# First two columns in one load, first up matmuls ahead of column 1's gate, other spin counts

## The chip, the cores and the metric

One core of a Trainium2 chip runs the kernel. The metric is device time in microseconds (us). The kernel before takes about 178.5 us. The profile's span starts and ends a little inside the measured time (176.9 of 178.62 us in one run).

Engine names: PE is TensorE, PEld its weight loads, DVE is VectorE, ACT ScalarE, POOL GpSimd, SP SyncE, whose queue ("SPq") issues nearly all loads.

## The reference, cut to what matters

```python
x  = A_x                                   # 1 x 2048 x 512, bf16
xn = _layernorm(x, axis=-1)
# A: rfft2, product with a complex weight, irfft2        (not touched here)
# B: h = gelu(xn @ w_gate) * (xn @ w_up);  h @ w_down    (512 -> 1792 -> 512)
return x + _A_ref(xn, A_w_r, A_w_i) + _B_ref(xn, B_w_gate, B_w_up, B_w_down)
```

The kernel works in 16 "columns" of 128 rows. A column is loaded, normalised and transposed; then gate and up matmuls take it through weights that are still arriving.

## The kernel before

The loads, in the order in which SyncE issues them:

```python
pin(load_x(0, 1))                  # column 0
pin(load_x(1, 1))                  # column 1
idx_t = pc.tile([P, 3], I32, name="idx_t")
nc.sync.dma_start(out=idx_t[:], in_=nc.inline_tensor(idx_np, name="spec_rows").ap())  # index table
load_w(Wg_sb, 0, 512)              # first gate weights
load_w(Wu_sb, 0, 512)              # first up weights
load_x(2, 2)
for e in range(0, NE, 2):
    load_w(Wg_sb, 512, 1024, e=slice(e, e + 2))
load_w(Wu_sb, 512, 1024)           # second up block
load_x(4, 4)
# ... more weights, columns 8 to 15, tables
```

The index table is read by gathers late in the kernel. TensorE runs dummy matmuls ("spins") until there is work, so that its array is at full pace (in the trace spins start every 107 ns up to 4.87 us and every 56 ns from 5.86 us on):

```python
for k in range(37):
    pin(nc.tensor.matmul(sp_ps[:, :P], lhsT=spin[:], rhs=spin[:], start=True, stop=True))

def spin_on():                      # after column 0's transposes
    for k in range(11):
        nc.tensor.matmul(sp_ps[:, :P], lhsT=spin[:], rhs=x_t[:, 0, :P], start=True, stop=True)
```

The first units of work: `k == 0` is column 0 and `k == 1` column 1 with the first weights, `k == 2` and `k == 3` are both columns with the second block. `LAND`, `WG_LAND` and `WU_LAND` are landing times assumed by a list scheduler in the source; `key` orders the operations of an engine.

```python
if k == 0:
    g = add("PE", occ / 4, lambda: mm_part(0, 1), [xT_op[0, 0]], key=1000, acq=("G",), t_min=WG_LAND[0])
    between["t", 0].deps.append(g)                 # column 1's transposes come between
    g = add("PE", occ / 4, lambda: mm_part(1, 2), [g, between["t", 1]], key=1000.1)
    g = add("PE", occ / 2, lambda: mm_part(2, NE), [xT_op[0], g], key=1000.2, lat=occ / 2 + 0.3)
# ...
u = split("u_ps", "U", Wu_sb, (1001.4, 1001.5, 1003.1, 1003.5)[k] if k < 4 else 1000.5 + k, WU_LAND, ...)
```

So TensorE's order was: gate of column 0 (with column 1's transposes inside), gate of column 1, up of column 0, up of column 1, then 256-wide gate matmuls for both columns, transposes of columns 2 and 3, 256-wide up matmuls.

## Time and profile before

| | before |
|---|---|
| time, median of 3 runs | 178.56 us (178.42 to 178.85) |
| PE busy | 172.8 of 176.9 us |
| first gate matmul | 6.66 us |
| first 256-wide gate matmul | 10.47 us |
| last matmul | 173.93 us |

The page's first part gives each engine's busy time, its share of the span and its instructions:

```profile
span 176.9 us, 3143 instructions
## 1 busy us (share of the span) xinstructions
PE 172.8 (98%) x1150; PEld 96.9 (55%) x1150; DVE 115.9 (66%) x255; ACT 96.0 (54%) x171; POOL 17.2 (10%) x38
```

PE has almost no idle time left, so a gain has to come from the few us before the real matmuls start. The timeline of PE from 5 us shows them; columns are start, length, engine, line, operation, tiles, shapes and count, and in brackets the idle time before with what ended it:

```profile
...
5.42 0.61 PE L351 MATMUL tp<-ident_t,xn 128*128 128x128 bf16 x4 [0.24 <-DVE xn L345]
5.86 0.78 PE L324 MATMUL sp_ps<-x_t,spin 128*128 128x128 bf16 x11
6.66 0.40 PE L502 MATMUL g_ps<-xnT,Wg_sb 128*128 128x128 bf16 x4
6.90 0.39 PE L351 MATMUL tp<-ident_t,xn 128*128 128x128 bf16 x4
7.12 1.73 PE L502 MATMUL g_ps<-xnT,Wg_sb 128*128 128x128 bf16 x28
...
```

The waits of PEld name what the first gate weights waited for (total us, times, longest):

```profile
PEld L320 <- DVE minus_half L266: 1.0, 1, 1.0
PEld L351 <- DVE xn L345: 0.7, 2, 0.5
PEld L502 <- DMA Wg_sb<-in_B_w_gate_dram: 0.2, 1, 0.2
```

The reader should see two chains that race to 6.66 us: column 0 (load, statistics, normalise, transposes, spins) and the landing of the gate weights. The weights lost, by 0.2 us: the last spin starts at 6.42 us and the first gate matmul, 0.045 us behind the landing of its weights, at 6.66.

### The profile page before, as it was taken

The numbers are of one execution on the slowest core, as the hardware profiler recorded it, in microseconds if no ns is written. First come the engines' busy times: TensorE is split into PE (matmuls) and PEld (weight loads), VectorE is DVE, ScalarE is ACT, GpSimd is POOL, SyncE is SP. The second block draws the span as 40 slices with busy tenths as digits, with TensorE's granted clock in tenths as the row PEclk, the third lists the DMA queues.
The fourth block names the chain that finished last, engine by engine and source line by source line (L and its number), as shares of the span: only waits on it lengthen the run. The fifth ranks groups of instructions, "written<-read, shape, count | busy, mean of one in ns | idle before, by whom it ended". The sixth has DMA issues, their size and how long they took to land.

```text
span 176.9 us, 3143 instructions
## 1 busy us (share of the span) xinstructions
PE 172.8 (98%) x1150; PEld 96.9 (55%) x1150; DVE 115.9 (66%) x255; ACT 96.0 (54%) x171; POOL 17.2 (10%) x38
## 2 busy tenths in 40 slices
PE   7999999999999999999999999999999999999993
PEld 7798845455545554555555455454445445444463
DVE  2588999987434599979899999643516325345333
ACT  3452489799736988898899965362112111211200
POOL 1020340506760000000000000000000000000000
DMA  3999999233717802211201510200122221221212
GB/s 99 323 387 377 371 199 151 60 64 71 246 41 238 299 0 59 59 30 35 59 19 42 152 47 15 59 0 4 59 89 89 77 75 60 89 88 60 82 40 59
DMA packets 21743, 19.35 MB, mean 109 GB/s; under 512 B 8480, under 2 KB 20000, under 8 KB 21728
## 3 DMA queue, kind: packets, MB, share of 16 engines
q1 hardware_dynamic: 21312, 17.84, 36.4%
q0 software_dynamic: 416, 1.32, 2.6%
q8 instruction: 9, 0.15, 0.4%
q14 instruction: 6, 0.05, 0.1%
HBM read 13.38 MB, written 2.10 MB: 87 GB/s over the span
## 4 chain that ended last, share of the span: by engine, by line
PE 95%; DVE 2%; DMA 1%; issue 0%
PE u_ps L494 27%; PE y_ps L829 27%; PE g_ps L494 25%; PE g_ps L502 2%; PE bp L589 2%; PE yp L780 2%; PE gp L750 2%; PE dp L647 2%; PE y_ps L833 2%; PE ep L656 2%; DMA x_t<-in_A_x_dram 1%; DVE stats L339 1%; PE tp L351 1%; DVE xn L345 0%; DVE xnT L354 0%; DVE y_sb L836 0%
## 5 line engine op out<-in xcount | busy, mean ns | idle before, releaser
L494 PE MATMUL u_ps<-xnT,Wu_sb 128*128 128x512 bf16 (+2 forms) x272 | 57.1, 341 | 0.0
L494 PE MATMUL g_ps<-xnT,Wg_sb 128*128 128x512 bf16 (+1 forms) x224 | 53.3, 364 | 0.0
L829 PE MATMUL y_ps<-Wd_sb,hT 128*128 128x512 bf16 (+2 forms) x252 | 51.1, 355 | 0.0
L512 DVE TENSOR_TENSOR hT<-u_ps,ge 128x512 bf16<-128x512 f32 x56 | 38.4, 688 | 18.1 <-PE u_ps L494 16.5
L507 ACT ACTIVATE ge<-g_ps 128x512 bf16<-128x512 f32 x56 | 33.5, 601 | 22.3 <-PE g_ps L494 18.3
L494 PEld LDWEIGHTS <-Wu_sb 128*128 128x128 bf16 x272 | 24.8, 98 | 20.7
L829 PEld LDWEIGHTS <-hT 128*128 128x128 bf16 x252 | 23.2, 98 | 22.4
L494 PEld LDWEIGHTS <-Wg_sb 128*128 128x128 bf16 x224 | 21.5, 98 | 20.5
L786 ACT CAST yf<-yp 128x512 bf16<-128x512 f32 x16 | 9.3, 586 | 40.5 <-PE yp L780 40.5
L836 DVE TENSOR_TENSOR y_sb<-y_ps,y_sb 128x512 bf16<-128x512 f32 (+2 forms) x18 | 11.1, 632 | 30.0 <-PE y_ps L833 30.0
L661 ACT CAST E<-ep 64x512 bf16<-64x512 f32 x32 | 18.5, 579 | 1.4 <-PE ep L656 1.0
L339 DVE BATCH_NORM_STATS2 stats<-x_t 128x6 f32<-128x512 bf16 x16 | 10.4, 674 | 3.9 <-DMA x_t<-in_A_x_dram 3.9
L456 ACT ACTIVATE xn<-x_t,nb,rstd 128x512 bf16<-128x512 bf16 x12 | 9.5, 812 | 1.0 <-POOL nb L370 1.0
L559 ACT CAST ds<-dp 128x512 bf16<-128x512 f32 x16 | 9.2, 597 | 0.8 <-PE dp L647 0.8
L559 ACT CAST Gs<-gp 128x512 bf16<-128x512 f32 x16 | 8.7, 591 | 0.6 <-PE gp L750 0.5
L559 ACT CAST Bs<-bp 128x512 bf16<-128x512 f32 x16 | 8.3, 606 | 0.5 <-PE bp L589 0.5
L792 DVE TENSOR_TENSOR lv<-yf 128x512 bf16<-128x512 bf16 x16 | 6.1, 421 | 1.5 <-ACT yf L786 0.6
L780 PEld LDWEIGHTS <-Gs 128*128 128x128 bf16 x64 | 4.8, 98 | 3.5
L799 DVE TENSOR_TENSOR yt<-lv 128x512 bf16<-128x512 bf16 x16 | 6.1, 421 | 0.3
L833 PE MATMUL y_ps<-yt,RI_t 128*128 128x512 bf16 (+2 forms) x18 | 6.1, 355 | 0.0
L780 PE MATMUL yp<-CT,Gs 128*128 128x128 bf16 x64 | 6.0, 219 | 0.0
L571 DVE TENSOR_TENSOR A<-xn 128x1024 bf16<-128x1024 bf16 x8 | 5.2, 676 | 1.0 <-ACT xn L456 1.0
(65 smaller groups left out, 125.5 us busy)
## 6 DMA issues: line engine op xcount, KB each, us to landing
F<-F SPq DMA_DIRECT2D x32, 64.0 KB, 2.0
y_sb<-in_A_x_dram SPq DMA_DIRECT2D x16, 128.0 KB, 2.1
out_dram<-y_sb SPq DMA_DIRECT2D x15, 128.0 KB, 1.7
Wd_sb<-in_B_w_down_dram SPq DMA_DIRECT2D x1, 1792.0 KB, 7.6
x_t<-in_A_x_dram SPq DMA_DIRECT2D x5, 256.0 KB, 9.8
Wu_sb<-in_B_w_up_dram SPq DMA_DIRECT2D x2, 512.0 KB, 6.2
Wg_sb<-in_B_w_gate_dram SPq DMA_DIRECT2D x1, 768.0 KB, 10.2
Wu_sb<-in_B_w_up_dram SPq DMA_DIRECT2D x1, 768.0 KB
```

Of the source, the lines that this page charges most:

```text
L339: V.bn_stats(out=st[:], in_=x_t[:, c, :])
L456: xn_op[c] = add("ACT", 0.72, lambda c=c: A.activation(out=xn[:, c, :], in_=x_t[:, c, :], func=AF.Identity, bias=nb[:, c:c + 1], scale=rst ...
L494: T_.matmul(b[name][:, f], lhsT=W_[:, e, (f0 + f) * P:(f0 + f + 1) * P], rhs=rhs[:, e, :], start=(e == 0), stop=(e == NE - 1))
L507: A.activation(out=b["ge"][:], in_=b["g_ps"][:], func=AF.Gelu_apprx_tanh)
L512: V.tensor_tensor(out=hT_of(sb, f0, m, o, w), in0=b["u_ps"][:], in1=b["ge"][:], op=ALU.mult)
L559: A.copy(out=o, in_=i)
L661: A.copy(out=b["E"][64 * h:64 * h + 64, r], in_=b["ep", h][64 * r:64 * r + 64])
L780: T_.matmul(t[:, q], lhsT=late["G"][:, q, c0 + j], rhs=IQ[q], start=(q == 0), stop=(q == 3), skip_group_check=True)
L786: A.copy(out=b["yf"][:, j], in_=b[j][:])
L829: T_.matmul(b[o][:], lhsT=hT_of(sb, f, 1, cl * P, P)[:, 0], rhs=Wd_sb[:, f, o:o + w], start=(f == 0), stop=False)
L833: T_.matmul(b[o][:], lhsT=late["RI"][:, c, :], rhs=late["yt"][:, c, o:o + w], start=False, stop=True)
L836: V.tensor_tensor(out=b["y"][:, o:o + w], in0=b[o][:], in1=b["y"][:, o:o + w], op=ALU.add)
```

## The change: its intent and its diff

The intent: one issue fewer ahead of the weights, so that index table and weights go out earlier, and an order that uses the first up weights as soon as they are expected.

```diff
-    pin(load_x(0, 1))
-    pin(load_x(1, 1))
+    pin(load_x(0, 2))
...
-    load_x(4, 4)
+    load_x(4, 2)
+    load_x(6, 2)
...
-    LAND = {0: 2.7, 1: 3.4, 2: 8.55, 3: 8.55}
+    LAND = {0: 2.95, 1: 2.95, 2: 8.2, 3: 8.2}
-    WG_LAND = [6.1] * 4 + [10.15] * 4 + [13.2] * 6
-    WU_LAND = [7.6] * 4 + [11.7] * 4 + [15.2] * 6
+    WG_LAND = [5.7] * 4 + [9.8] * 4 + [13.2] * 6
+    WU_LAND = [7.15] * 4 + [11.3] * 4 + [15.2] * 6
...
-    for k in range(37):
+    for k in range(40):
...
-        for k in range(11):
+        for k in range(6):
...
-            g = add("PE", occ / 4, lambda: mm_part(0, 1), [xT_op[0, 0]], key=1000, acq=("G",), t_min=WG_LAND[0])
+            g = add("PE", occ / 2, lambda: mm_part(0, 2), [xT_op[0, 0]], key=1000, acq=("G",), t_min=WG_LAND[0])
+            g = add("PE", occ / 4, lambda: mm_part(2, 3), [xT_op[0], g], key=1000.01)
             between["t", 0].deps.append(g)
-            g = add("PE", occ / 4, lambda: mm_part(1, 2), [g, between["t", 1]], key=1000.1)
-            g = add("PE", occ / 2, lambda: mm_part(2, NE), [xT_op[0], g], key=1000.2, lat=occ / 2 + 0.3)
+            g = add("PE", occ / 4, lambda: mm_part(3, NE), [g, between["t", 1]], key=1000.2, lat=occ / 4 + 0.3)
...
-        u = split("u_ps", "U", Wu_sb, (1001.4, 1001.5, 1003.1, 1003.5)[k] ...
+        u = split("u_ps", "U", Wu_sb, (1000.5, 1001.5, 1003.1, 1003.5)[k] ...
```

The resulting order of matmuls, before and after, counted:

```
before: 37 spins, 4 transposes (col 0), 11 spins, 4 gate, 4 transposes (col 1), 28 gate, 32 up,
        16 gate 256-wide, 8 transposes (cols 2, 3), 16 up 256-wide, ...
after:  40 spins, 4 transposes (col 0),  6 spins, 12 gate, 4 transposes (col 1), 4 gate, 16 up, 16 gate, 16 up,
        12 gate 256-wide, 4 up 256-wide, 8 transposes (cols 2, 3), 4 up, 4 gate, 8 up 256-wide, ...
```

More of the change, by code (lines that the diff above doesn't have):

```diff
@@ L410, in first_two @@
         T(0, 1)
-        add("PE", 0.61, spin_on, [o["T", 0, 1]], key=-1500, lat=0.61, after=o["T", 0, 1])
+        add("PE", 0.33, spin_on, [o["T", 0, 1]], key=-1500, lat=0.33, after=o["T", 0, 1])
         table = add("ACT", 1.3, lambda: None, [o["root", 1]], key=-1500, lat=1.3)
@@ L535, in unit @@
             g = split("g_ps", "G", Wg_sb, 1000 + k, WG_LAND, m)
-        u = split("u_ps", "U", Wu_sb, (1001.4, 1001.5, 1003.1, 1003.5)[k] if k < 4 else 1000.5 + k, WU_LAND, (2, m, 1)[k] if k < 3 else m)
+        u = split("u_ps", "U", Wu_sb, (1000.5, 1001.5, 1003.1, 1003.5)[k] if k < 4 else 1000.5 + k, WU_LAND, (2, m, 1)[k] if k < 3 else m)
         ge = add("ACT", {1: 0.28, 2: 0.36, 4: 0.5}[n * m], f_ge, [g], key=-1000 + k,
```

## The prediction

> What bounds the kernel now. The profile's first part gives TensorE (PE) 172.8 of 176.9 us; the granted clock is 1.00 in every window I read. The waits of PE list one item after its start, 0.2 us, and the chain of waits is PE almost end to end from 6.68 us on. So the span is: the start of the gate matmuls (6.66 us), a stream of matmuls without a gap to 174 us, a tail of about 2.8 us. Only the first 6.7 us can give anything, if the stream stays closed behind it.
>
> Who sets that start: in the timeline the spins on column 0 have their last start at 6.42 us, then PE idles 0.2 us; its weight load is released by the landing of the first gate weights (issued 2.18, landed 6.62). The data side (column 0 landed 3.40, stats 3.43, transposes 5.42, copy to 6.03) is ready earlier; column 1 (normalised at 6.67) is just in time.
>
> What the change does.
> 1. One load for columns 0 and 1: one issue fewer on SyncE. An issue there costs 0.42 to 0.47 us from start to start, so index table, gate and up weights, columns 2 and 3 go out 0.46 us earlier. Between 2.1 and 4.1 us the DMA engines are busy 0.67 of the time, so these transfers are not yet bound by bandwidth, and I expect landings 0.4 to 0.46 us earlier: gate weights 6.62 -> 6.2, up weights 8.05 -> 7.6, columns 2-3 9.01 -> 8.6, second up block 12.0 -> 11.6.
> 2. Against that, column 0 comes with column 1 (alone they landed at 3.40 and 3.70): I estimate 3.6, so the VectorE chain starts 0.2 us later: transposes at 5.6, copy done at 6.25.
> 3. Spins: 37 -> 40 of 0.107 us (filling up to the later transposes), 11 -> 6 of 0.056 us after them. The six end at about 6.4 us, which now releases the first gate matmul: 0.25 us earlier than before.
> 4. Order: after 16 gate matmuls and 4 transposes (20 x 0.056 = 1.1 us) come column 0's 16 up matmuls, at about 7.53 us, ahead of column 1's gate. They need the up weights, at about 7.6 plus release: a new gap of 0.1 us. Before, they began at 8.63, with 0.6 us in hand. So the stream ends about 0.17 us earlier.
> 5. The other order changes (part of the second up matmuls ahead of transposes 2 and 3, columns 4-7 in two loads) open no wait that I find: up block two lands about when it is wanted (11.6), a gap under 0.1 us. From 14 us on the PE order is the same.
>
> The Trainium skill ("TensorE: Matmul & The Clock Gate", Part 1) says back-to-back N=128 matmuls take 106.7 ns cold and 55.6 ns warm, warm after about 3.4 us busy. The trace agrees: 106.7 ns from 1.1 to 4.9 us, 56 ns from 5.4 us.
>
> Result: 0.1 to 0.3 us out of 178.56; no more than the spread of the three runs (178.42 to 178.85). Predicted 178.38 us, 8 in 10 between 178.05 and 178.75. Faster by over 2%: 0.01; within 2%: 0.98; slower by over 2%: 0.01.
>
> What would show it: gate weights landing near 6.2, first gate matmul at 6.35 to 6.5; column 0's stats at 3.55 to 3.7; a small PE wait on the up weights at 7.5 to 7.7; the first 128x256 gate matmul at 10.2 to 10.35 (before 10.47); PE closed after it, tail unchanged.
>
> What would make it wrong: the pair of columns landing much later (over 3.8); the weights not following their earlier issue, because the larger load is ahead of them; the clock dropping in the gaps, at 107 ns a matmul; an engine order that opens a gap at transposes 2 and 3.

## The result, and the profile after

| | before | after |
|---|---|---|
| time, median of 4 runs each | 178.53 us (178.42 to 178.85) | 178.58 us (178.42 to 178.89) |
| ratio, 95% interval | | 1.0002 (0.9982 to 1.0022) |
| first gate matmul in the trace | 6.66 us | 6.47 us |
| first 256-wide gate matmul | 10.47 us | 10.63 us |
| last matmul | 173.93 us | 174.01 us |

Ratios here and below are the mean time of one kernel's fast runs over that of the other's of the same rounds, so they are not quite the ratio of the medians. The number lies in the forecast range, but no gain shows.

The same lines of PE's timeline after the change:

```profile
5.69 0.61 PE L351 MATMUL tp<-ident_t,xn 128*128 128x128 bf16 x4 [0.74 <-DVE xn L345]
6.14 0.50 PE L324 MATMUL sp_ps<-x_t,spin 128*128 128x128 bf16 x6
6.47 0.83 PE L502 MATMUL g_ps<-xnT,Wg_sb 128*128 128x128 bf16 x12
7.14 0.39 PE L351 MATMUL tp<-ident_t,xn 128*128 128x128 bf16 x4
7.37 0.39 PE L502 MATMUL g_ps<-xnT,Wg_sb 128*128 128x128 bf16 x4
...
```

and the waits of PEld:

```profile
PEld L351 <- DVE xn L345: 1.1, 2, 0.9
PEld L320 <- DVE minus_half L266: 1.0, 1, 1.0
PEld L494 <- DMA Wu_sb<-in_B_w_up_dram: 0.4, 1, 0.4
```

The gate did start 0.19 us earlier than in the first trace, and the wait on gate weights is gone. In its place there is one of 0.4 us on the up weights. The last gate matmul of column 0 starts at 7.53 us, the first up matmul at 7.94 instead of 7.59, so 0.35 us are lost where 0.19 were won.

The chain of waits says the same. After, it reaches back from the up matmuls to the issue of their load (columns: start, us, what):

```profile
2.18 5.72 DMA Wu_sb<-in_B_w_up_dram
7.90 0.05 issue
7.94 1.07 PE u_ps L494 x16
```

Before, at that place, it ran through column 0's load and VectorE:

```profile
0.80 2.60 DMA x_t<-in_A_x_dram
3.40 0.02 issue
3.43 0.70 DVE stats L339
```

It is tempting to stop here: "the up matmuls were moved ahead and now wait". The experiments show that this is only a part.

One thing is needed to read them. The trace records when each of the sixteen parts of a load signals its landing. The Trainium skill ("DMA: Bandwidth & Descriptors", section "Why a DMA increments its semaphore by 16 and not by 1") says that a DMA runs on up to 16 engines that finish independently and that the semaphore counts them. This trace agrees: the sixteen parts of the up weights signalled from 6.64 to 7.90 us. The waiting engine sees only the last of them:

```
first up weights           8th part   15th part   16th part (us)
before, first trace          7.25        7.85        8.05
after,  first trace          6.83        7.18        7.90
```

The eighth part came 0.42 us earlier, as forecast; the last one 0.16 us.

### The profile page after: what moved, and what is told of

Same layout as the page of the kernel before. It is cut to its first block, busy times and chain, and to the rows that moved or that the text cites. A ratio compares the mean times of both kernels' runs of the same rounds, so it can differ in the third digit from the quotient of the medians.

```text
span 177.0 us, 3139 instructions
## 1 busy us (share of the span) xinstructions
PE 172.2 (97%) x1148; PEld 96.5 (55%) x1148; DVE 115.9 (65%) x255; ACT 96.4 (54%) x171; POOL 17.2 (10%) x38
## 4 chain that ended last, share of the span: by engine, by line
PE 94%; DMA 3%; SPq 1%; DVE 0%; issue 0%
PE u_ps L494 27%; PE y_ps L829 27%; PE g_ps L494 25%; DMA Wu_sb<-in_B_w_up_dram 3%; PE dp L647 2%; PE yp L780 2%; PE gp L750 2%; PE bp L589 2%; PE y_ps L833 2%; PE ep L656 2%; PE g_ps L502 1%; PE tp L351 0%; SPq L277 0%; SPq L283 0%; SPq L273 0%; DVE y_sb L836 0%
```

## The experiments

Theory A: what took the gain is the wait on the last part of the up weights, in the new order. Rival B: the joint load makes columns 0 and 1 later, and this took the gain; the order is harmless.

A device for reading all traces: from the first 256-wide gate matmul to the last matmul, every kernel here needs 163.37 us plus whatever gap is still open near 12 us. (After: 174.006 - 10.634 = 163.37. Before: 163.45, with the gap of 0.08 at the transposes.) So the positions of a few matmuls tell where the time went more sharply than the times do, whose spread is 0.5 us or more. The end is as regular: the measured time is 4.69 to 4.70 us more than the start of the last matmul in both traces of before and in both of the changed kernel, so a run's time tells, as an estimate, where its stream ended even when it was not profiled.

### a2_repeat: the changed kernel again

No edit.

> The changed kernel again, for a second trace. Theory A (the stream of matmuls now starts when the last sixteenth of the first up weights lands, 7.90 us in the first trace although the first fifteen were in by 7.18): the landing of the last sixteenth moves by some tenths of a us from run to run, the PE wait on the up weights with it, and the first 128x256 gate matmul (10.63 us in the first trace) stays 2.7 us behind that landing. Rival B (the joint load makes columns 0 and 1 0.27 us late, and that is what took the gain): the same times as in the first trace, whatever the up weights do. Time: same as before within 0.2%.

Measured: 178.69 us (178.37 to 179.01), ratio to before 1.0006 (0.9988 to 1.0025). In this trace column 0 landed at 3.80, and the first gate matmul started at 6.60. The up weights' last part was in at 7.71, and their first matmul followed at 7.76, with a gap of 0.04 us. The 256-wide gate started at 10.45, 2.7 us behind that landing as theory A had said. Then a second wait opened, on the second up block, whose last part landed at 12.19. PE's timeline there:

```profile
11.32 0.60 PE L502 MATMUL g_ps<-xnT,Wg_sb 128*128 128x256 bf16 x4
12.24 0.50 PE L494 MATMUL u_ps<-xnT,Wu_sb 128*128 128x256 bf16 x3 [0.31 <-DMA Wu_sb<-in_B_w_up_dram]
```

The last gate matmul ahead of it starts at 11.65. At their usual spacing of 0.109 us the next would have started at 11.76, so 0.48 us were lost. Theory A's landing jitter is there, and the new order has a second place where it bites. Before, that block was wanted at 12.75 and landed at 11.99, with 0.76 us in hand.

### e1_gate_first: the old order of gate and up, everything else changed

```diff
-    WU_LAND = [7.15] * 4 + ...
+    WU_LAND = [8.2] * 4 + ...
-        u = split(..., (1000.5, 1001.5, 1003.1, 1003.5)[k] ...
+        u = split(..., (1001.4, 1001.5, 1003.1, 1003.5)[k] ...
```

> The changed kernel with column 1's gate matmuls ahead of column 0's up matmuls again; loads and spins stay changed. Theory A: no PE wait on up weights (landed about 7.9, wanted at about 8.7); in its place a gap of about 0.2 us ahead of column 1's gate, whose transposed copy is ready only at about 7.75; first 128x256 gate matmul at 10.45 to 10.5, 0.15 us earlier than in the changed kernel's trace, so level with the kernel before (178.5 us). Rival B: no change against the changed kernel, 10.6 us.

Measured: 178.77 us, ratio 1.0028 (1.0004 to 1.0052; one of its six runs took 179.83), so if anything slower than before. The gap moved as forecast: none on the up weights (landed 7.56, used at 8.77), but column 1's gate waits from 7.62 to 7.88 for its transposed copy. The 256-wide gate is at 10.56, where theory A had said 10.45 to 10.5. Undoing this part of the order does not bring the gain back. It does not show B either: column 1 was normalised at 7.03, and its transposes start at 7.23, right behind the twelfth gate matmul (7.17). So the new gap comes for the most part from the place of these transposes, behind 12 gate matmuls instead of 4, which e1 left changed.

### e2_order_only: only the new order, on the kernel before

```diff
-        u = split(..., (1001.4, 1001.5, 1003.1, 1003.5)[k] ...
+        u = split(..., (1000.5, 1001.5, 1003.1, 1003.5)[k] ...
```

> The kernel before with the one new order alone: column 0's up matmuls ahead of column 1's gate; loads, spins and the split of the gate matmuls as before. Theory A: up matmuls are ready to run at about 7.8 us and the up weights land at about 8.05, so a wait of 0.25 to 0.3 us, and the time is about 0.25 us over the kernel before (178.8). Rival B: no change (within 0.05 us), as columns 0 and 1 land as before.

Measured: 178.49 us (178.34 to 178.58), ratio 0.9999 (0.9981 to 1.0017). The trace has the wait (last gate matmul 7.30, first up matmul 7.72, weights landed 7.68), so 0.36 us are lost at that place. But the time is level with before, against theory A's 178.8. The interval is 0.3 us wide on either side, so this run alone does not exclude a small cost. The trace also shows something else: with exactly the loads of before, its first gate matmul started at 6.23 us, not 6.66, again right behind its weights, which landed at 6.18:

```profile
6.22 0.23 PEld L502 LDWEIGHTS <-Wg_sb 128*128 128x128 bf16 x4 [0.23 <-DMA Wg_sb<-in_B_w_gate_dram]
```

### e3_joint_load: only the joint load, on the kernel before

```diff
-    pin(load_x(0, 1))
-    pin(load_x(1, 1))
+    pin(load_x(0, 2))
```

> The kernel before with columns 0 and 1 in one load alone; spins 37 and 11, order as before. Both theories: stats on column 0 at 3.70 instead of 3.43; gate weights land near 5.7 to 6.2, no longer the release; the 11 spins end at about 6.75, the first gate matmul starts there (before 6.66). Theory A: stream closed from there, first 128x256 gate matmul at 10.57, time +0.1 us. Rival B: column 1 opens further gaps, 10.7 us or later, time +0.25 us or more.

Measured: 178.77 us, ratio 1.0016 (0.9998 to 1.0034): unclear, but on the side of slower. Column 0 landed at 3.55, gate weights at 5.87, the first gate matmul started at 6.63, behind the spins; the 256-wide gate at 10.475, with no other gap. So the gate is released by the chain of column 0, and the weights, now 0.76 us ahead of it, no longer matter.

### e7_up0_on_gate and e8_up02_on_gate: take the waits on up weights away

In e7 column 0's up matmuls read the gate weights, in e8 also the first of the second block. Their outputs are wrong, which doesn't matter for the times. (The comparison with the reference did not notice it.) Order and instructions are those of the changed kernel.

```diff
-        u = split("u_ps", "U", Wu_sb, (1000.5, ...
+        u = split("u_ps", "U", Wg_sb if k == 0 else Wu_sb, (1000.5, ...        # e7
+        u = split("u_ps", "U", Wg_sb if k in (0, 2) else Wu_sb, (1000.5, ...   # e8
```

> The changed kernel with column 0's first up matmuls reading the gate weights (a wrong result on purpose): the same instructions in the same order, but the up weights are first wanted only by column 1, near 9.4 us. Theory A (PE waits for the last sixteenth of the up weights): the gap at 7.5 us is gone, the first 128x256 gate matmul comes 3.8 us behind the first gate matmul, at 10.3 us; up block two then is wanted at about 11.6 and lands at 11.5 to 12.2, so a part of the gain, 0 to 0.35 us of it, is lost there again. Rival B (columns 0 and 1 being late): the gap stays and the 128x256 gate matmuls start at 10.45 to 10.65.

> As e7, and the first up matmuls of the second block read gate weights too (wrong result on purpose). Theory A with both waits: neither gap is there, PE is closed from the first gate matmul (about 6.5) to 14 us, and the time is 0.3 to 0.4 us under the changed kernel (about 178.25). Rival B: no better than the changed kernel (178.6).

Measured: e7 178.70 us, ratio 1.0013 (0.9997 to 1.0030); e8 178.51 us, ratio 0.9997 (0.9984 to 1.0009); before in the same rounds 178.63. In e7 the first gap is gone, as theory A says, and the second wait takes the time back:

```profile
11.98 0.33 PEld L494 LDWEIGHTS <-Wu_sb 128*128 128x128 bf16 x4 [0.41 <-DMA Wu_sb<-in_B_w_up_dram]
```

In e8 both are gone and PE is closed from 6.53 us on. Yet e8 only draws level with before; 178.25 had been expected. So the waits on up weights cost the changed kernel something like 0.1 to 0.2 us (178.51 against 178.58, 178.69 and 178.70, from different rounds), and with all of them removed the change still gains nothing. What is left in e8 is the chain from the joint load to the first gate matmul:

```profile
0.80 2.94 DMA x_t<-in_A_x_dram
3.74 0.02 issue
3.76 0.70 DVE stats L339
4.47 0.02 issue
4.49 0.18 DVE mv L342
```

That is rival B, as far as the start is concerned: the spins behind the transposes, and no longer the gate weights (6.36), release the first gate matmul (6.53).

### e9_index_late_only and e6_index_late: save the same issue without joining the columns

e9 moves the index table's load, which is not needed early, behind columns 8 and 9. The weights go out 0.46 us earlier, exactly as in the changed kernel, and columns 0 and 1 stay separate. (The table's own transfer, 1.5 KB, is out of the way as well; the runs do not tell its effect from that of the issue.) e6 adds 5 spins in place of 11 and a division of column 0's gate into 8 matmuls, column 1's transposes, 8 matmuls.

```diff
-    idx_t = pc.tile([P, 3], I32, name="idx_t")
-    nc.sync.dma_start(out=idx_t[:], in_=nc.inline_tensor(idx_np, name="spec_rows").ap())
 ...
     load_x(8, 2)
+    idx_t = pc.tile([P, 3], I32, name="idx_t")
+    nc.sync.dma_start(out=idx_t[:], in_=nc.inline_tensor(idx_np, name="spec_rows").ap())
```

```diff
# e6, on top of e9 (and landing times of the list scheduler to match)
-        for k in range(11):
+        for k in range(5):
 ...
-            g = add("PE", occ / 4, lambda: mm_part(0, 1), ...
+            g = add("PE", occ / 2, lambda: mm_part(0, 2), ...
             between["t", 0].deps.append(g)
-            g = add("PE", occ / 4, lambda: mm_part(1, 2), ...
-            g = add("PE", occ / 2, lambda: mm_part(2, NE), [xT_op[0], g], ...
+            g = add("PE", occ / 2, lambda: mm_part(2, NE), [xT_op[0], g, between["t", 1]], ...
```

> The kernel before with the index table's load moved back alone. Theory A: weights land about 0.4 us earlier, the 11 spins (last start 6.42) and no longer the gate weights release the first gate matmul, at 6.45 to 6.5 (6.85 to 7.0 if the array is still slow then); the rest closed; 0 to 0.2 us under the kernel before.

> The kernel before with the index table's load moved behind columns 8 and 9 (columns 0 and 1 in two loads, as before), 5 spins on column 0 in place of 11, the first 8 gate matmuls ahead of column 1's transposes, up matmuls behind column 1's gate as before. Weights go out 0.46 us earlier and columns 0 and 1 are not delayed. Theory A: first gate matmul at 6.1 to 6.3, no wait on the first up weights (landed near 7.7, wanted at 8.3), first 128x256 gate matmul at 10.05 to 10.2, and up block two wanted at 11.9 just about when it lands: 0.2 to 0.4 us under the kernel before (178.2). Rival B: the same, since columns 0 and 1 are as before; so this tells how much an earlier start can give at all.

Measured: e9 178.26 us, ratio 0.9980 (0.9967 to 0.9993); e6 178.21 us, ratio 0.9975 (0.9962 to 0.9988); before 178.63. Both beat before by a little, with intervals that exclude 1. The saved issue is worth about 0.35 us when it is not paid for with column 0. e9's trace, from the slowest of its five runs, shows 10.37 for the 256-wide gate; e6's shows 10.20 with the gate weights landing late, at 6.35.

### b2_before_again and e6b_index_late: how typical were the traces?

No edits.

> The kernel before again, for a second trace. If its first gate matmul (6.665 us in the first trace, released by the last sixteenth of the gate weights at 6.62) moves with that landing, it is anywhere between 6.2 and 6.7 here (the kernel with the new order alone, with the same loads, had 6.23), and the last matmul starts 167.2 to 167.3 us behind it. If the first trace was typical, 6.6 to 6.7.

> e6_index_late again. If its gain is real: 0.2 to 0.45 us under the kernel before once more, first 128x256 gate matmul at 10.0 to 10.3, no wait on up weights. If it was a lucky chip or round: level with before.

Measured: before again 178.37 us (178.04 to 178.67), ratio to the other runs of before 0.9999; e6 again 178.09 us, ratio 0.9977 (0.9961 to 0.9992). The gain of e6 was found twice, on two chips. In the second trace of before the first gate matmul started at 6.15 us and the last at 173.38:

```profile
0.80 2.15 DMA x_t<-in_A_x_dram
2.95 0.03 issue
2.98 0.70 DVE stats L339
```

Column 0 landed at 2.95 here, against 3.40 in the trace on which the forecast was built. But the release was once more the landing of the gate weights: 6.10, with the first gate matmul 0.047 us behind it, while the last spin had started at 5.97. This run took 178.08 us and is one of the quicker of its kernel; the first trace's, at 178.62, was somewhat slower than the mean of 178.48 (43 runs of before).

e6b's trace also shows why starting still earlier gives so little. Its first gate matmul is at 5.87 and its 256-wide gate at 9.67, 0.29 us ahead of the second trace of before. Then PE waits for columns 2 and 3:

```profile
11.61 0.55 PEld L351 LDWEIGHTS <-xn 128*128 128x128 bf16 x8 [0.31 <-DVE xn L345]
```

Their load landed at 8.43; after statistics and root, column 2 is normalised from 11.14 to about 11.55. The 256-wide up matmuls start at 12.17 us, against 12.20 in the second trace of before.

### e10_late_up_first: the new order on top of e6

```diff
-    WU_LAND = [8.2] * 4 + ...
+    WU_LAND = [7.15] * 4 + ...
-        u = split(..., (1001.4, 1001.5, 1003.1, 1003.5)[k] ...
+        u = split(..., (1000.5, 1001.5, 1003.1, 1003.5)[k] ...
```

> e6 with column 0's up matmuls ahead of column 1's gate matmuls, nothing else. Theory A: PE waits for the up weights (landed 7.7 to 8.0, wanted 1.1 us behind the first gate matmul, at 7.3 to 7.5): 0.2 to 0.5 us lost against e6, so about level with before. Rival B (the order costs nothing, columns set the pace): level with e6.

Measured: 178.02 us, ratio to before 0.9980 (0.9965 to 0.9995), against 178.09 and 0.9977 for e6b in the same rounds: the order costs nothing that can be seen (the means of six runs each differ by 0.03 us, give or take 0.2). The wait itself is there:

```profile
7.26 0.84 PEld L494 LDWEIGHTS <-Wu_sb 128*128 128x128 bf16 x15 [0.31 <-DMA Wu_sb<-in_B_w_up_dram]
```

but the 256-wide up matmuls start at 12.15, where they start in e6b (12.17) without it. PE waits 0.3 us for up weights at 7 us in one order, and 0.3 us for columns 2 and 3 at 11.5 us in the other. Theory A's cost of 0.2 to 0.5 us is not there with these early loads: the wait is real, but in these two traces it only takes the place of a later one.

### e11_late_joint: the joint load on top of e6

```diff
-    pin(load_x(0, 1))
-    pin(load_x(1, 1))
+    pin(load_x(0, 2))
```

> e6 with columns 0 and 1 in one load, nothing else; the weights go out another 0.46 us earlier. Rival B holds for this part: column 0 lands at about 3.7 instead of 2.95 to 3.4, its transposes are at 5.7 instead of 5.0 to 5.4, the first gate matmul at 6.3 to 6.4 is released by the spins or the column's copy and no longer by the weights, column 1's transposes open a gap of 0.1 to 0.2 us: 0.1 to 0.3 us over e6. Theory A alone (only the up weights matter): level with e6 or better by up to 0.2 us, as the weights are earlier.

Measured: 179.73 us (178.97 to 180.72), ratio to before 1.0086 (1.0051 to 1.0121): 1.6 us over e6b's median, worse than B had forecast. Column 0 landed at 4.28 us, with the weights' load issued right behind it, and PE stood idle (this kernel's line numbers are one less):

```profile
6.30 0.61 PE L350 MATMUL tp<-ident_t,xn 128*128 128x128 bf16 x4 [1.12 <-DVE xn L344]
```

The first gate matmul is at 7.02, 1.16 us behind e6b's. The six times fall in two groups, 179.0 to 179.1 and 180.4 to 180.7. The trace is of a run of 179.11; what the slower three do stays open.

## Why the prediction was right or wrong

The landings in all traces but e11's, last part, and below them the start of the first gate matmul, us (joint: the changed kernel twice, e1, e3, e7, e8; separate columns: before twice, e2; index late: e9, e6, e6b, e10):

```
                           separate            joint                                  index late
column 0                   3.40 2.95 2.93      3.68 3.80 3.68 3.55 3.79 3.74          3.42 2.96 2.93 2.95
first gate weights         6.62 6.10 6.18      5.66 5.93 5.84 5.87 6.00 6.36          6.52 6.35 5.82 5.73
first up weights           8.05 7.57 7.68      7.90 7.71 7.56 7.89 8.04 7.78          7.91 7.79 7.30 7.22
second up block           11.99 11.77 11.70    11.70 12.19 11.79 11.47 11.94 11.96    11.75 11.49 11.50 11.38
first gate matmul          6.66 6.15 6.23      6.47 6.60 6.56 6.63 6.58 6.53          6.56 6.39 5.86 5.78
```

The last line shows what the change does to the start. With separate columns, in all seven traces, the first gate matmul starts 0.045 to 0.047 us behind the landing of its weights: the weights set the start. With the joint load, in all six, the weights are there 0.18 to 0.81 us before it, and it starts one spacing (0.056 us) behind the last spin: column 0's chain sets the start.

- Where the time is bounded. Right. PE is closed behind the start, and all differences come from the first 13 us.
- Step 1, "landings 0.4 to 0.46 us earlier". Right for the gate weights alone: the mean goes from 6.30 to 5.94. The first up weights do not come earlier (7.77 to 7.81), nor does the second up block (11.82 to 11.84). From 4.1 us on the DMA engines are busy throughout (share 1.04 from 4.1 to 6.5 us, before and after). The gap at 2.1 to 4.1 us, on which the step rested (0.67 before, 0.77 after), seems to help only the transfers that fit into it; that this is the reason was not tested. With separate columns and the index table late, up weights and second block do come earlier, at 7.56 and 11.53 in the mean. Part of these differences is between chips: on the chip of e6 to e9 the up weights landed at 8.04 and 7.78 with the joint load and at 7.91 and 7.79 with the index table late, which is no clear difference. On another chip, however, e11 issued its up weights 0.47 us earlier than e6b did (1.71 against 2.18) and got them 0.34 us later (7.64 against 7.30).
- Step 2, "the VectorE chain starts 0.2 us later". The landing was nearly right: 3.6 was forecast, and the joint load lands at 3.71 in the mean. What it was compared with was not. Column 0 alone lands at 3.08 in the mean of the seven traces with separate columns; five of them are within 2.93 to 2.96. So the landing is 0.6 us later, three times the forecast. Not all of this reaches the start, since with separate columns the chain of column 0 was waiting for the weights anyway, by 0.07 to 0.22 us where the 11 spins were kept. The 3.40 of the first trace was one of two late landings in seven. The size fits the packets: in the first trace the 128 packets of column 0 took 58 ns each, in the changed kernel the 128 packets of twice the size 99 ns. With eight on each of sixteen engines, the estimate is 8 x 0.041 = 0.33 us more, and the eighth part's landing does move by about that much, from 2.77 (first trace) to 2.98 (changed) and 3.03 (changed again). The rest is the last parts' lateness; why that is larger in the joint load was not found.
- Step 3, "the six end at about 6.4 us, which now releases the first gate matmul: 0.25 us earlier than before". The mechanism is right: the spins release it in both traces of the changed kernel, 2.79 and 2.80 us behind column 0's landing, where the forecast has 2.8. The gain is not there. With the changed loads and spins the start is at 6.47, 6.60, 6.56, 6.58 and 6.53 (changed twice, e1, e7, e8), mean 6.55 and not 6.41, mostly because column 0 lands 0.1 us later than forecast. And the 6.66 of the first trace was taken as the kernel's start, whereas the traces with the loads of before have 6.66, 6.15 and 6.23. Three starts that far apart give no sure mean, but the times help: in the two traces of before the time is 171.93 to 171.96 us more than the start, so the mean of 178.48 puts the usual start near 6.54, as an estimate for runs without other gaps. By the same reckoning the runs of e8 start at 6.64 and those of before in the same rounds at 6.65. So the start is about level.
- Step 4, "a new gap of 0.1 us" at the up weights. The mechanism is right, and the size was 0.35 us in one trace and nothing in the other. It hardly decides the time: e8 without it is at most 0.2 us better, and e10 against e6b shows no cost.
- Step 5, "no wait that I find" and "a gap under 0.1 us" at the second up block. Wrong: 0.48 us in a2 and, by the same reckoning, about 0.3 in e7; none in the first trace.
- The clock. The slow pace ended ahead of the first gate matmul in all traces. The latest was relative to its gate in e1, where the spins behind the transposes were slow until 6.28 us; from the last transpose to the first gate matmul it took 0.45 us, against 0.39 in the changed kernel.

In sum, the number was right because the forecast gain was about as small as the noise; that it fell into the range says little for the steps. The term that should have made the gain, the gate starting earlier, came to about nothing: the weights are 0.36 us earlier in the mean of the traces, but the joint load hands the start over to column 0, whose chain ends at about the time at which the weights used to land. What remains in the changed kernel is the same start and one wait or the other on up weights. How much each part costs below 0.2 us could not be settled by these times.

## What to carry to other kernels

A load's landing is that of its slowest part, and one trace is one draw from it. Before a race between two chains of similar length is costed (here gate weights against column 0, with 0.07 to 0.22 us between them), it takes several traces, or the spread of the parts in one. To let weights go out earlier, move a load that nobody needs early out of their way (here the index table: one moved load, 0.2%), instead of fusing it with a load that the first chain waits for. And where several loads bound the same stream one behind the other, ask what each would allow alone: removing the nearest wait gives only the distance to the next.

## What the Trainium skill lacked or had wrong

- "DMA: Bandwidth & Descriptors", section "Why a DMA increments its semaphore by 16 and not by 1", states that the parts finish independently but does not say how far apart. Here the sixteenth part followed the fifteenth by 0.01 us (up weights, second trace of before: 7.56 and 7.57) to 0.77 us (gate weights, e9: 5.74 and 6.51).
- The same page, section "Anatomy of one DMA — SWDGE (gpsimd) path", fits 2.0 us plus bytes over 436 KB per us. For 128 and 256 KB that is 2.30 and 2.60 us, an estimate from the page, whose fit is for another issuing path. Here, with further loads in flight, they took 2.13 to 2.62 us and 2.75 to 3.00 us (3.5 in e11): doubling cost 0.6 us in the mean, not 0.3.
- "TensorE: Matmul & The Clock Gate", Part 1, puts the change from the slow to the fast pace at around 4 us of activity, give or take 0.5. With spins from 1.05 us on, the fast pace began at 3.76 in e6b, at 4.29 in the changed kernel's first trace and at 6.28 in e1, so after 2.7, 3.2 and 5.2 us (with two pauses of 0.4 and 0.2 us in the last). The paces themselves, 107 and 56 ns, agree.
- No page says that an earlier issue need not give an earlier landing when the DMA engines are full behind it: first up weights issued 0.47 us earlier landed at 7.81 instead of 7.77 us in the mean (six traces against three, not all on one chip).
